# Two-layer transformer kernel: second-layer key chunks of 3, 4, 4, 3, 2 tiles, clock-keeping filler in dead score banks, and one key tile in sixteen exponentiated on VectorE

## The chip, the cores and the metric

The kernel runs on one core of a Trainium2 chip. Every time is device time in microseconds (us) of one execution; a kernel's time is the median of its runs. A profile is one further execution, so its span differs a little from the median.

Names: PE is TensorE's matrix multiplications, PEld its weight loads, DVE is VectorE, ACT is ScalarE, POOL is GpSimd. PSUM is the memory that TensorE writes (eight banks of 512 fp32 columns); SBUF is the memory beside all engines. PV stands for the product of the probabilities with the values.

## The reference, cut to what matters

```python
def _A_ref(x, wqkv, wo):                 # S = 2048 rows, D = 448, 16 heads of 28
    q, k, v = split_heads(x @ wqkv)
    scores = einsum("bhqd,bhkd->bhqk", q, k) * (28 ** -0.5)
    return merge_heads(einsum("bhqk,bhkd->bhqd", softmax(scores), v)) @ wo

def _B_ref(x, w1, w2, w3, w4):
    h = gelu(layernorm(x) @ w1)          # 448 wide, then shifted by rows -1, +1, -2, +2
    x1 = x + shifted(h) @ w2
    return x1 + gelu(layernorm(x1) @ w3) @ w4      # 1792 wide

x = A_x
x = x + _A_ref(layernorm(x), ...);  x = x + _B_ref(layernorm(x), ...)
x = x + _A_ref(layernorm(x), ...);  x = x + _B_ref(layernorm(x), ...)   # same weights again
```

Two layers with the same weights. The second layer's attention needs keys from every row of the first layer's output, so there is a **seam**: the second layer can only begin on the keys that the first layer's MLP has already finished.

## The kernel before: the parts that the change and the argument touch

The work is written as tasks (Python generators), one per stage. When the program is built, a small planner simulates them with estimated durations and priorities and so fixes one order of instructions for each engine. Each engine is given its list in that order, and the profiles show it: in those of the changed kernel and of runs 5 and 6, the 1230 instructions of VectorE, the 882 of ScalarE and the 394 of GpSimd come in one and the same order.

```python
def c_ps(n): return 0.07 + n * 0.00104        # planner's estimate: VectorE, n columns from PSUM;
                                              # used for four of the five operations of t_dexp too

# rows are cut in 16 tiles of 128. (first tile, tiles) of the query chunks, and per layer the
# order of the segments: (query chunk, from key tile, to key tile)
CHUNKS = {0: [(0,4),(4,4),(8,4),(12,4)], 1: [(0,4),(4,4),(8,4),(12,2),(14,2)]}
ORDER = {0: [(0,0,4),(0,4,8),(0,8,16),(1,0,16),(2,0,16),(3,0,16)],
         1: [(0,0,4),(0,4,8),(1,0,8),(0,8,12),(1,8,12),(0,12,16),(1,12,16),
             (2,0,16),(3,0,16),(4,0,16)]}     # each times 4 head groups of 4 heads

def DVE_TILES(L, ch, g, p): return 0          # key tiles of a segment exponentiated on VectorE
def MIXP(L, ch): ...                          # priority of a query chunk's out-projection and MLP
def KVP(L, c): ...                            # priority of a key chunk's projections; low = early
```

A **block** is one head, one tile of 128 keys and up to 512 queries: one PSUM bank. ScalarE takes two or three blocks in one exponential. `t_dexp` is the same thing on VectorE; it was in the kernel before, but its list was empty:

```python
def t_exp():                                                   # ScalarE
    for u, un in enumerate(units):
        yield ("wait", ("st", u))                              # scores are in PSUM
        if u >= 6:                                             # its PT slot is read by PV of unit u-6
            for (si, kb, j) in units[u - 6]: yield ("wait", ("pv", si, kb))
        yield op("act", 0.07 + n * 0.427, ... activation(out=PT[...], in_=ps[...], func=ACT.Exp, scale=SCALE))
        ...
def t_dexp(w):                                                 # VectorE: exp by exponent bits and a cubic
        ...
        b = yield ("acq", MISC, [("yd", w)])                   # one of the spare PSUM banks
        yield from score_ops([blk], [bi(b)])
        op("dve", ... tensor_scalar(out=y, in0=ps[:, bi(b), :], ..., op0=ALU.mult, op1=ALU.max))
        op("dve", ... scalar_tensor_tensor(out=q, in0=lo, ..., in1=lo, ...))    # lo, hi: halves of y
        op("dve", ... scalar_tensor_tensor(out=q, in0=q, ..., in1=lo, ...))
        op("dve", ... tensor_scalar(out=pd, in0=q, ..., op0=ALU.mult, op1=ALU.add))
        op("dve", ... scalar_tensor_tensor(out=pd, in0=hi, scalar=128.0, in1=pd, ...))
        ...
def t_pv():                                                    # one PSUM bank (5), one segment at a time
    for si in range(len(segs)):
        if si > 0: yield ("wait", ("ucopied", si - 1))         # bank 5 copied out
        while todo or dtodo:
            if dtodo and (not todo or <its VectorE blocks are done>):  ... read PD
            else:                                                      ... read PT
```

The keys of a chunk pass through projection, a square (ScalarE for the very first, GpSimd otherwise), a sum and a maximum; from the maximum comes the **bias** that keeps the exponentials in range. A segment with new keys waits for that bias.

```python
fast = L == 0 and c == 0 and g == 0                            # square on ScalarE
...
def keep_pe_busy(self, until):                                 # filler between two PE instructions
    dur, fn, banks, key, reads = self.fill                     # banks: ["b6", "b7"], the spare ones
    while self.cur["pe"] + dur + 0.12 < until:
        used = <planned TensorE work in the last WIN us>
        if used > self.TARGET * self.WIN: ...continue          # quota reached
        for b in banks:
            if self.busy.get(b, False): continue
            ...
        self.P.add("pe", <small matmul into bank b>)
```

## Time and profile before

The three runs took 1208.27 us (1207.6 to 1210.52).

| | span us | ScalarE busy | exponentials | VectorE busy | GpSimd busy | mean granted clock |
|---|---|---|---|---|---|---|
| before | 1202.5 | 1059.7 | 819, 939.3 us | 452.2 | 382.7 | 0.956 |

The prediction below shows the rows that name the bound. Three more lines of the page matter later: VectorE's row of the 40 slices, the score matmuls, and GpSimd's normalisation. A group's line ends in its busy time, the mean ns of one instruction, the idle time of its engine before it, and what ended most of it.

```profile
DVE  8464213331242235331643353423352433233243
...
L1138 PE MATMUL ps<-qT,kT 32*128 32x512 bf16 (+1 forms) x2304 | 326.5, 368 | 52.2 <-ACT PT L1213 43.6
...
L850 POOL TENSOR_SCALAR xn<-x_res,mv,mst 128x448 bf16<-128x448 f32 x30 | 55.6, 1865 | 1.9 <-DVE mst L1451 1.9
```

VectorE is far from full (most slices 1 to 5 tenths). The score matmuls wait mostly for an exponential to release their bank (43.6 of 52.2 us), which is what a ScalarE bound looks like from TensorE. The windows view of the stretch at the seam gives each engine's busy time in 45 us (columns: PE, PEld, DVE, ACT, POOL, granted clock, DMA share, GB/s); ScalarE works only 26.65 of them:

```profile
690.00:735.00 45.00, 39.88 (x462) 15.29 (x455) 23.36 (x58) 26.65 (x25) 12.19 (x13) 0.93 0.20 61
```

### The profile page before, as it was taken

How to read it: one execution, taken by the hardware profiler on the slowest of the kernel's cores; microseconds unless marked ns; L12 is line 12 of the kernel's file. 1: busy time of each engine (PE TensorE's matmuls, PEld its weight loads, DVE VectorE, ACT ScalarE, POOL GpSimd, SP SyncE). 2: the span in 40 equal slices, each digit the busy share in tenths (PEclk: the TensorE clock that was granted, in tenths of full speed). 3: DMA queues.
4: the chain of work that ended last, by engine and by line, in shares of the span. 5: the costliest groups of instructions: out<-in, count | busy, mean ns of one | idle time of the engine just before them, and what ended most of it. 6: DMA issues, size and time to landing. Idle time of an engine off the chain costs nothing.

```text
span 1202.5 us, 34008 instructions
## 1 busy us (share of the span) xinstructions
PE 1058.9 (88%) x15542; PEld 417.7 (35%) x15542; DVE 452.2 (38%) x921; ACT 1059.7 (88%) x906; POOL 382.7 (32%) x396
## 2 busy tenths in 40 slices
PE   5998888889888899898988998988889898889888
PEld 2333333343323332223332433332323433334355
DVE  8464213331242235331643353423352433233243
ACT  3768999999989999989999958998989999899932
POOL 4931114403325054412343240202427501252201
PEclk9899999899979999998998999998999998899899
DMA  3384112002111032011231021324321110220000
GB/s 102 83 242 103 38 51 46 15 17 71 27 30 29 11 107 46 11 19 48 75 94 35 20 90 44 106 89 112 60 38 35 26 45 22 45 47 11 10 17 22
DMA packets 95784, 64.28 MB, mean 53 GB/s; under 512 B 64664, under 2 KB 84440, under 8 KB 95640
## 3 DMA queue, kind: packets, MB, share of 16 engines
q1 hardware_dynamic: 92376, 57.63, 19.2%
q0 software_dynamic: 2304, 3.67, 1.2%
q8 instruction: 122, 2.00, 0.7%
q10 hardware_dynamic: 960, 0.80, 0.2%
q14 instruction: 22, 0.18, 0.1%
HBM read 28.16 MB, written 16.76 MB: 37 GB/s over the span
## 4 chain that ended last, share of the span: by engine, by line
ACT 40%; PE 37%; DMA 8%; DVE 7%; POOL 5%; issue 1%; SPq 0%; ACTq 0%; POOLq 0%; DVEq 0%
ACT PT L1213 34%; PE ps L706 21%; PE ps L1138 9%; PE ps L697 6%; DMA rb<-rscr 4%; ACT h2T L1604 3%; POOL xn L850 2%; DMA xT<-xnd 1%; POOL otn L1357 1%; ACT hT L1488 1%; DMA rscr<-rT 1%; PE ps L1643 1%; DVE kmaxc L981 1%; DMA rT<-ub 1%; ACT L1604 1%
## 5 line engine op out<-in xcount | busy, mean ns | idle before, releaser
L1213 ACT ACTIVATE PT<-ps 128x1536 bf16<-128x1536 f32 (+1 forms) x819 | 939.3, 1307 | 59.2 <-PE ps L1138 56.6
L1138 PE MATMUL ps<-qT,kT 32*128 32x512 bf16 (+1 forms) x2304 | 326.5, 368 | 52.2 <-ACT PT L1213 43.6
L697 PE MATMUL ps<-PT,vaug 128*32 128x512 bf16 (+1 forms) x2304 | 254.1, 367 | 2.0 <-DVE ub L1335 2.0
L1138 PEld LDWEIGHTS ps<-qT,kT 32*128 32x128 bf16 x2304 | 80.3, 91 | 342.6 <-ACT PT L1213 271.7
L1643 PE MATMUL ps<-wq_pad,ident 128*32 128x256 bf16 x3836 | 182.4, 282 | 2.1 <-DVE x1b L1547 1.0
L706 PE MATMUL ps<-xT,w 128*32 128x512 bf16 (+1 forms) x2240 | 173.2, 367 | 6.9 <-issue 4.7
L706 PE MATMUL ps<-w,h2T 128*32 128x448 bf16 x1792 | 123.5, 382 | 20.8 <-ACT h2T L1604 20.8
L1357 POOL TENSOR_TENSOR otn<-ub,rb 128x512 bf16<-128x512 f32 (+1 forms) x32 | 38.6, 1205 | 320.6 <-DMA rb<-rscr 314.1
L1643 PEld LDWEIGHTS ps<-wq_pad,ident 128*32 128x32 bf16 x3836 | 108.9, 98 | 43.3 <-issue 23.8
L1594 DVE CAST h2T<-ps 128x512 bf16<-128x512 f32 (+2 forms) x126 | 73.9, 586 | 121.0 <-PE ps L706 112.6
L697 PEld LDWEIGHTS ps<-PT,vaug 128*32 128x32 bf16 x2304 | 69.8, 95 | 102.1 <-issue 85.4
L706 PEld LDWEIGHTS ps<-xT,w 128*32 128x32 bf16 x2240 | 59.0, 96 | 63.8 <-issue 38.1
L706 PEld LDWEIGHTS ps<-w,h2T 128*32 128x32 bf16 x1792 | 49.7, 102 | 68.6 <-issue 27.3
L850 POOL TENSOR_SCALAR xn<-x_res,mv,mst 128x448 bf16<-128x448 f32 x30 | 55.6, 1865 | 1.9 <-DVE mst L1451 1.9
L958 POOL TENSOR_TENSOR sq<-qT 128x512 bf16<-128x512 bf16 x31 | 32.1, 1040 | 73.0 <-DVE qT L1001 68.8
L850 POOL TENSOR_SCALAR xn<-x1b,mv,mst 128x448 bf16<-128x448 f32 x29 | 54.5, 1879 | 1.7 <-POOL mst L1553 0.2
L1333 DVE COPY ub<-ps 128x512 f32<-128x512 f32 (+1 forms) x36 | 22.7, 630 | 85.4 <-PE ps L697 85.2
L958 POOL TENSOR_TENSOR sq<-kT 128x512 bf16<-128x512 bf16 x31 | 32.2, 1041 | 66.6 <-DVE kT L970 63.5
L706 PE MATMUL ps<-w,hT 112*32 112x448 bf16 x512 | 40.9, 414 | 13.8 <-ACT hT L1488 13.5
L706 PE MATMUL ps<-xT,wq_pad 128*32 128x512 bf16 x512 | 44.8, 420 | 6.2 <-DMA xT<-xnd 5.5
L706 PE MATMUL ps<-wo_pad,otn 128*32 128x448 bf16 x512 | 42.0, 378 | 9.1 <-POOL otn L1357 6.1
L1604 ACT ACTIVATE h2T<-h2T 128x7168 bf16<-128x7168 bf16 (+2 forms) x9 | 45.1, 5015 | 3.9 <-DVE h2T L1594 3.8
(134 smaller groups left out, 869.4 us busy)
## 6 DMA issues: line engine op xcount, KB each, us to landing
uscr<-ub SPq DMA_DIRECT2D x28, 256.0 KB
ub<-uscr SPq DMA_DIRECT2D x28, 256.0 KB
rb<-rscr SPq DMA_DIRECT2D x28, 256.0 KB
xnd<-xn SPq DMA_DIRECT2D x28, 128.0 KB, 2.0
x_res<-in_A_x_dram POOLq DMA_DIRECT2D x16, 224.0 KB, 3.5
xd<-x_res SPq DMA_DIRECT2D x16, 224.0 KB, 2.1
x_res<-xd SPq DMA_DIRECT2D x16, 224.0 KB
out_dram<-obf SPq DMA_DIRECT2D x16, 112.0 KB
```

Source lines behind the costliest of these rows:

```text
L697: return lambda e: e.matmul(out=out, lhsT=lhsT, rhs=rhs, start=start, stop=stop, **kw)
L706: r.append(e.matmul(out=out[c:c + w, :], lhsT=lhsT[:, c:c + w], rhs=rhs, start=start, stop=stop, tile_position=(0, c)))
L850: yield op(eng, dur, lambda e: e.tensor_scalar(out=xn[:, k, 0:D], in0=src, scalar1=scalar1, scalar2=scalar2, op0=ALU.subtract, op1=ALU.mul ...
L958: return op("pool", 1.2, lambda e: e.tensor_tensor(out=sq[:, si, :], in0=src, in1=src, op=ALU.mult), reads=rk, writes=[("sq", si)])
L981: yield op("dve", c_ps(512), lambda e: e.reduce_max(out=kmaxc[:, L, g, c:c + 1], in_=ps[:, bi(b2), :], axis=AX.X), reads=[("ps", bi(b2))], ...
L1138: yield op("pe", max(0.055, 0.22 / nc_ * NW / 512.0), lambda e, i=i, kc=kc, j=j, g=g, a=a, NW=NW, bank=bank: e.matmul(out=ps[:, bank, i * ...
L1213: yield op("act", 0.07 + n * 0.427, lambda e, bk=bk, s0=s0, n=n: e.activation(out=PT[:, s0:s0 + n, :], in_=ps[:, bk[0]:bk[0] + n, :], func ...
L1333: yield op("dve", c_ps(NW), lambda e: e.tensor_copy(out=u, in_=ps[:, 5, 0:NW]), reads=[("ps", 5)], writes=[uk])
L1357: yield op("pool", 0.2 + NW * 0.0021, lambda e: e.tensor_tensor(out=otn[:, g, 0:NW], in0=u, in1=rb[:, 0:NW], op=ALU.mult), reads=[uk, ("rb ...
L1594: ev = op("dve", c_ps(NW), lambda e, fch=fch, b=b: e.tensor_copy(out=h2T[:, fch, 0:NW], in_=ps[:, bi(b), 0:NW]), reads=[("ps", bi(b))], wr ...
L1604: yield op("act", c_act(14 * NW), lambda e: e.activation(out=h2T[:, :, 0:NW], in_=h2T[:, :, 0:NW], func=ACT.Gelu_apprx_tanh), reads=allk, ...
L1643: return [e.matmul(out=ps[32 * c:32 * c + 32, bi(b), 0:256], lhsT=ident[:, 32 * c:32 * c + 32], rhs=wq_pad[:, 0, 0:256], start=True, stop= ...
```

## The change

It aims at ScalarE from several sides: fewer exponentials for it (VectorE takes one key tile in sixteen of each full segment), earlier keys at the seam (chunks that end where the MLP's groups of tiles end, and new priorities), a better clock (filler in more banks), a shorter start (first squares on ScalarE), and planner estimates nearer to the trace. The core of the diff:

```diff
-    WIN = 3.42                          # filler window and quota
-    TARGET = 0.5
+    WIN = 2.3
+    TARGET = 0.52
-                if self.busy.get(b, False):
+                if b not in self.dead:
-        SC.fill = (0.12, filler, ["b6", "b7"], ...)
+        SC.fill = (0.12, filler, ["b6", "b7", "b0", "b1", "b2", "b3", "b4"], ...)

 def DVE_TILES(L, ch, g, p):
-    return 0
+    return {16: 1}.get(p, 0)

 MIXP: -(0, 3): 1.6                      +(0, 3): 1.4
 KVP:  -(1, 1): 1.5, (1, 2): 1.5         +(1, 1): 2.5, (1, 2): 2.5, (1, 4): 1.5

-        return 0.07 + n * 0.00104       # c_ps
+        return 0.13 + n * 0.00108
 # ... and small VectorE operations estimated at 0.2 instead of 0.1 or 0.12

-  1: [(0,0,4),(0,4,8),(1,0,8),(0,8,12),(1,8,12),(0,12,16),(1,12,16),(2,0,16),...]
+  1: [(0,0,7),(1,0,7),(0,7,11),(1,7,11),(0,11,16),(1,11,16),(2,0,16),...]
+    KC = {0: [(0,4),(4,4),(8,4),(12,4)], 1: [(0,3),(3,4),(7,4),(11,3),(14,2)]}
 # ... projections, squares and maxima take 128 * n columns instead of 512

-            fast = L == 0 and c == 0 and g == 0
+            fast = L == 0 and c == 0
-            if idx == 0 and g == 0:     # the same for the first queries' squares
+            if idx == 0:
 # ... banks b4 and b3 are left out of the general list until the tail (MISC[0:3]); a query projection
 #     waits for its bias before it takes a bank; bookkeeping of dead banks cut
```

## The prediction

> **What bounds the kernel now.** The median is 1208.27 us; the profiled execution spans 1202.5 us. I read the page first, then the groups of instructions, then ScalarE's timeline, then the waits and the PE timeline around ScalarE's gaps.
>
> ```profile
> span 1202.5 us, 34008 instructions
> PE 1058.9 (88%) x15542; PEld 417.7 (35%) x15542; DVE 452.2 (38%) x921; ACT 1059.7 (88%) x906; POOL 382.7 (32%) x396
> ACT  3768999999989999989999958998989999899932
> PEclk9899999899979999998998999998999998899899
> L1213 ACT ACTIVATE PT<-ps 128x1536 bf16<-128x1536 f32 (+1 forms) x819 | 939.3, 1307 | 59.2 <-PE ps L1138 56.6
> L1643 PE MATMUL ps<-wq_pad,ident 128*32 128x256 bf16 x3836 | 182.4, 282 | 2.1 <-DVE x1b L1547 1.0
> ```
>
> TensorE and ScalarE look equally full at 88%, but 182.4 us of TensorE is filler (line 1643) that only keeps its clock up. ScalarE does no filler: 939.3 of its 1059.7 us are the softmax exponentials of line 1213. In the ACT row most slices are 9s; the holes are the start (3, 7, 6), the 5 in slice 24 (690 to 720 us) and the last two slices. So ScalarE is the bound, with 1202.5 - 1059.7 = 142.8 us idle.
>
> The price of an exponential comes from a long undisturbed stretch, and the largest hole from the same view, ScalarE's timeline (start, duration, line, shapes, count, idle before and its releaser):
>
> ```profile
> 683.35 1.28 ACT L1604 ACT_TABLE_LOAD   x1
> 684.64 4.68 ACT L1604 ACTIVATE h2T<-h2T 128x5376 bf16<-128x5376 bf16 x1
> ...
> 694.26 13.94 ACT L1213 ACTIVATE PT<-ps 128x1536 bf16<-128x1536 f32 x12 [1.26 <-PE ps L1138]
> 722.52 0.20 ACT L1113 ACTIVATE fct<-dbc 128x4 f32<-128x4 f32 x1 [14.32 <-DVE dbc L1108]
> 723.63 4.86 ACT L1213 ACTIVATE PT<-ps 128x1536 bf16<-128x1536 f32 x4 [0.91 <-PE ps L1138]
> ...
> 783.88 0.27 ACT L1113 ACTIVATE fct<-dbc 128x4 f32<-128x4 f32 x1
> ...
> 1055.32 63.50 ACT L1213 ACTIVATE PT<-ps 128x1536 bf16<-128x1536 f32 x56
> ```
>
> The last line: 63.50 us for 56 exponentials, 1.134 us each. They alternate between 3 and 2 blocks (a block is one head, one tile of 128 keys, 512 queries), so 2.5 on average: **0.4536 us a block**. The 14.32 us line is the seam between the layers: ScalarE has run out of second-layer keys and waits for the bias step of a new key chunk.
>
> **What the skill says.** (1) "ScalarE: Activation LUTs", section What ACT_TABLE_LOAD costs, gives 0.833 ns per element; a block of 512 would then be 0.427 us plus its part of a fixed cost. The 0.4536 us agrees, and its table load of about 1283 ns is the 1.28 us line. (2) "VectorE: DVE Perf Modes", section Why PSUM operands drop a tier: fp32 read from PSUM runs at one element a cycle. The trace agrees: 512 columns from PSUM take 691 ns (the h2T cast of line 1594), where a bf16 scalar op inside SBUF takes 347 ns (line 1160). (3) "TensorE: Matmul & The Clock Gate", section Part 1: idleness of about 3.4 us drops the clock to half. The trace shows that after a gelu:
>
> ```profile
> 547.08 3.77 PE L1643 MATMUL ps<-wq_pad,ident 128*32 128x256 bf16 x124
> 554.24 5.42 PE L706 MATMUL ps<-w,h2T 128*32 128x448 bf16 x56 [3.39 <-ACT h2T L1604]
> 559.59 0.45 PE L1138 MATMUL ps<-qT,kT 32*128 32x512 bf16 x3
> ```
>
> The filler planned over the 7.5 us of table load and gelu runs off in 3.77 us, TensorE idles 3.39 us, and the granted clock in 556 to 560 us is 0.53.
>
> **The change part by part.**
>
> *One key tile in sixteen on VectorE.* It holds for segments of 16 key tiles whose query chunk is 4 tiles wide: chunks 1, 2, 3 of layer one and chunk 2 of layer two (chunks 3 and 4 there are 2 wide and excluded). That is 4 chunks x 4 head groups = 16 segments, each with 1 key tile x 4 heads: 64 of the 2048 blocks (2 x 16 heads x 16 key tiles x 4). ScalarE loses 64 x 0.4536 = **29.0 us**, and its 819 exponentials become about 794 (1984 / 2.5). This lies on the bound nearly everywhere: from 165 to 290 us ScalarE is busy 122 of 125. VectorE pays five operations a block: one from PSUM (0.69), three two-tensor ones inside SBUF (0.70 to 0.74, as the neighbours on lines 1027 and 1335), one fp32 to bf16 scalar op (about 0.42, between 347 ns and the PSUM price), together about 3.25 us. 64 x 3.25 = 208 us, so VectorE goes from 452 to about 660 us. In 290 to 430 us it is busy 39 of 140; 16 blocks add 52, giving 65%. It stays beside ScalarE. The score matmul uses the row group that a 3-block unit leaves free. The price is coupling: a block holds one of the two spare PSUM banks, projections wait for VectorE behind 0.7 us operations, and the last PV of a segment waits for the chain. I put that at one VectorE operation, about 0.6 us, per segment: 16 x 0.6 = **+10 us**.
>
> *Key chunks of 3, 4, 4, 3, 2 tiles.* The first layer's MLP finishes tiles in groups 0-2, 3-6, 7-10, 11-13, 14-15. Now chunk 2 is tiles 8 to 11, so it waits for the group of 11-13, whose gelu ends at 689 us. ScalarE has only 256 blocks (64 + 64 + 128) to do before that. The new chunks end where the groups end: 2 x 7 x 16 + 2 x 4 x 16 = 352 blocks need nothing from the last query chunk. Between 690 and 735 us ScalarE is busy 26.65 of 45: 18.35 us idle, which this part attacks. But the new order needs keys 11 to 15 together, all five chunks, and earlier in the work. First-layer exponentials end at about 575 us (the 410th). 352 x 0.4536 = 159.7 us, plus three gelu interruptions in that stretch (4.5, 7.3, 5.8), bring ScalarE to 752 us; the bias of the last keys came at 784 us. The chain must become 32 us shorter. The priorities help: the last chunk's MLP goes from 1.6 to 1.4 while second-layer key projections go from 1.5 to 2.5, so the out-projection (598 to 612 us, amid key and query work) and the last MLP groups no longer stand behind them, and the last key step is 2 tiles instead of 4 (765 to 784 us). I estimate 25 of the 32 us, so a new stall of about 7: net **-11 us**. Segments of layer two go from 40 to 36; those in the short round have 20 blocks instead of 16, so the normalisation chain behind it (rb from DRAM, 824 to 880 us, 11 us of ScalarE idle) gets more room: **-3 us**.
>
> *Filler in dead score banks, window 2.3 us.* Filler may use any bank whose contents are dead, instead of only the two spare ones. The gaps after gelu stay: the filler there has reached its quota already, and its quota rises only from 50 to 52%. Gaps from a late transpose DMA (TensorE waits 2.8 us for xT at 827 us, then runs at half clock) are not filler's to mend, as the planned DMA times are unchanged. I give it **-4 us**. It is also needed because the VectorE blocks occupy the two banks filler used.
>
> *Start.* All four head groups of the first chunk square on ScalarE instead of three of them on GpSimd (1.04 us each, six in all). ScalarE is idle 26 us between 23.6 and 109 us, so the six squares (6 x 0.6 = 3.6 us busy) fit, and they shorten the wait of 10.92 us at 25 us by about 3: **-3 us** of span.
>
> *VectorE cost estimates* are nearer to the trace (0.69 for 512 columns from PSUM instead of 0.60); they cost nothing and make the order fit better. I give them no number.
>
> Sum: -29 + 10 - 11 - 3 - 4 - 3 = **-40 us: 1168 us**.
>
> **Rivals.** (a) *VectorE becomes a second bound.* For it: second-layer chunk 2 has its blocks where VectorE is already busy 30.6 of 65 us (880 to 945); with 52 us over some 120, it reaches about 85%, and every PSUM evacuation queues. Against it: only one stage is so full. If it held, half of the 29 us would come back: about 1185 us. (b) *The seam moves instead of closing.* If the chain to keys 11-15 does not get shorter, ScalarE stalls 32 us at one point instead of 18 spread out: 14 us worse than before, so 1193 us. For it: much of that chain is latency (GpSimd normalising four tiles, 7.4 us; transpose DMAs). Against it: the priorities were retuned for it. (c) *Everything falls in place*: seam fully hidden, coupling near zero, filler removes half of the 39 us of small waits for scores: -29 - 18 - 3 - 15 - 3 = -68, 1140 us.
>
> **Range and chances.** (a) and (c) stand about as far off on either side; (b) is the worst single one. I take 1143 to 1193. Faster by over 2% means under 1184.1 us: the 29 us saved on ScalarE alone reach 1179, so only a new wait prevents it: 0.79. Within 2%: 0.18; slower: 0.03.
>
> **What would show it.** ScalarE: about 794 exponentials, total busy about 1034 us. VectorE about 660 us, still with idle time in each stage. The seam: no wait of 14 us on the bias near 700 us, and at most a short one before the (11-16) segments. Granted clock dips still after gelus. The prediction is wrong if ScalarE's idle time grows above 143 us: then look for waits of score matmuls on VectorE, or PV matmuls on the VectorE blocks, in chunks 1 to 3 of layer one.

## The result, and the profile after

The changed kernel took **1162.23 us** (1159.99 to 1165.16), with a ratio of **0.9629** to the kernel before (95% interval 0.9586 to 0.9672): faster. Ratios here are the mean time of one kernel's fast runs over that of the other's of the same rounds, so they are not quite the ratio of the medians quoted. In another session, on a kernel before of 1206.37 us, the same kernel took 1162.77 us at 0.965.

The page of the changed kernel, first the span, then the engines' busy times, three rows of the 40 slices, the exponentials and the filler:

```profile
span 1158.2 us, 33576 instructions
PE 1028.3 (89%) x15190; PEld 404.7 (35%) x15193; DVE 642.4 (55%) x1230; ACT 1026.0 (89%) x882; POOL 400.6 (35%) x394
...
DVE  7754237775677786756663424513658764333352
ACT  4958999999899999797799999899989999999922
PEclk9989999999899999999999999999989999999999
...
L1233 ACT ACTIVATE PT<-ps 128x1536 bf16<-128x1536 f32 (+2 forms) x794 | 906.1, 1322 | 53.4 <-PE ps L1158 37.7
...
L1665 PE MATMUL ps<-wq_pad,ident 128*32 128x256 bf16 x3416 | 155.6, 277 | 7.0 <-DVE yd L1269 3.2
```

ScalarE is still the fullest engine that does no filler. It has 33.7 us less work (1059.7 to 1026.0), but only 10.6 us less idle time (142.8 to 132.2). The ACT row has new holes in slices 17, 19 and 20 (7 where 9 stood, between 463 and 579 us); they are the subject of most of what follows. VectorE's row more than doubled between slices 7 and 20 (the digits add up to 91 instead of 41).

The seam, from ScalarE's timeline (start, duration, line, count, in brackets the idle time before and its releaser). The small exponential `fct` is the step behind the bias of the last keys:

```profile
748.43 0.20 ACT L1133 ACTIVATE fct<-dbc 128x4 f32<-128x4 f32 x1 [4.02 <-DVE dbc L1128]
749.54 48.48 ACT L1233 ACTIVATE PT<-ps 128x1024 bf16<-128x1024 f32 x43 [0.90 <-PE ps L1158]
```

The 14.32 us wait of before is gone; one of 4.02 + 0.90 us remains.

To see where the time went I count exponentials in each trace and so cut it into phases: the first 128 blocks; the rest of the first layer; the split segments of the second layer (query chunks 0 and 1); its full segments; and the tail after the last exponential. In us, each row from the one profiled execution of its kernel:

| kernel | first 128 blocks | rest of layer 1 | split segments | full segments | tail | span |
|---|---|---|---|---|---|---|
| before | 104.3 | 472.0 | 279.0 | 290.7 | 56.5 | 1202.5 |
| after | 100.7 | 457.9 | 264.8 | 272.1 | 62.7 | 1158.2 |
| after without VectorE tiles | 102.6 | 468.9 | 255.8 | 286.9 | 53.7 | 1167.9 |
| after with old key chunks | 101.8 | 463.5 | 276.5 | 269.3 | 62.3 | 1173.4 |
| after with old estimate | 98.6 | 466.6 | 260.5 | 283.3 | 63.7 | 1172.7 |
| after, no VectorE tiles in layer 1's last query chunk | 100.9 | 450.6 | 257.8 | 275.1 | 63.1 | 1147.5 |

In the rest of layer 1, VectorE took 48 blocks, which at the 0.4536 us of the prediction are 21.8 us of ScalarE; the phase shrank by 14.1. So a part of the gift was lost just there. How far one row may be trusted: a second profile of the changed kernel gave 100.3, 462.1, 264.7, 273.2 and 62.7, and the profiled execution of the kernel without VectorE tiles was the slowest of its four (1170.92 us; the others 1154.77 to 1165.07).

### The profile page after: what moved, and what is told of

It is laid out like the page before. It is cut to its first block, busy times and chain, and to the rows that moved or that the text cites. A ratio compares the mean times of both kernels' runs of the same rounds, so it can differ in the third digit from the quotient of the medians.

```text
span 1158.2 us, 33576 instructions
## 1 busy us (share of the span) xinstructions
PE 1028.3 (89%) x15190; PEld 404.7 (35%) x15193; DVE 642.4 (55%) x1230; ACT 1026.0 (89%) x882; POOL 400.6 (35%) x394
## 4 chain that ended last, share of the span: by engine, by line
ACT 54%; PE 26%; DVE 7%; DMA 6%; POOL 4%; SPq 1%; issue 1%; ACTq 0%; DVEq 0%
ACT PT L1233 47%; PE ps L720 14%; PE ps L1158 6%; PE ps L711 5%; ACT h2T L1626 3%; DMA rb<-rscr 2%; POOL xn L864 2%; ACT L1233 1%; ACT hT L1510 1%; DMA xT<-xnd 1%; DVE h2T L1616 1%; DMA rT<-ub 1%; POOL otn L1379 1%; DVE qd L1272 1%; ACT L1626 1%
## 5 line engine op out<-in xcount | busy, mean ns | idle before, releaser
L1233 ACT ACTIVATE PT<-ps 128x1536 bf16<-128x1536 f32 (+2 forms) x794 | 906.1, 1322 | 53.4 <-PE ps L1158 37.7
L720 PE MATMUL ps<-xT,w 128*32 128x512 bf16 (+2 forms) x2240 | 173.8, 365 | 8.2 <-DVE h2T L1616 2.3
L1665 PE MATMUL ps<-wq_pad,ident 128*32 128x256 bf16 x3416 | 155.6, 277 | 7.0 <-DVE yd L1269 3.2
L1379 POOL TENSOR_TENSOR otn<-ub,rb 128x512 bf16<-128x512 f32 (+1 forms) x32 | 40.4, 1262 | 267.5 <-DMA rb<-rscr 255.8
L1665 PEld LDWEIGHTS ps<-wq_pad,ident 128*32 128x32 bf16 x3416 | 93.3, 97 | 42.6 <-issue 18.6
L720 PEld LDWEIGHTS ps<-xT,w 128*32 128x32 bf16 (+1 forms) x2240 | 60.9, 96 | 64.6 <-issue 30.8
L864 POOL TENSOR_SCALAR xn<-x_res,mv,mst 128x448 bf16<-128x448 f32 x30 | 62.1, 2076 | 1.9 <-DVE mst L1473 1.5
L972 POOL TENSOR_TENSOR sq<-kT 128x512 bf16<-128x512 bf16 (+2 forms) x32 | 30.6, 957 | 89.9 <-DVE kT L986 76.7
L864 POOL TENSOR_SCALAR xn<-x1b,mv,mst 128x448 bf16<-128x448 f32 x29 | 57.2, 1973 | 1.7 <-POOL mst L1575 0.2
L1357 DVE SCALAR_TENSOR_TENSOR ub<-ub,fct,ps 128x512 f32<-128x512 f32 x24 | 17.9, 747 | 71.9 <-PE ps L711 69.9
L720 PE MATMUL ps<-xT,wk_pad 128*32 128x512 bf16 (+2 forms) x576 | 47.2, 375 | 6.8 <-DMA xT<-xnd 5.8
L1573 POOL TENSOR_SCALAR mst<-mv 128x1 f32<-128x1 f32 x32 | 8.0, 259 | 120.3 <-DVE mv L850 120.2
```

Source lines behind the costliest of these rows:

```text
L720: r.append(e.matmul(out=out[c:c + w, :], lhsT=lhsT[:, c:c + w], rhs=rhs, start=start, stop=stop, tile_position=(0, c)))
L864: yield op(eng, dur, lambda e: e.tensor_scalar(out=xn[:, k, 0:D], in0=src, scalar1=scalar1, scalar2=scalar2, op0=ALU.subtract, op1=ALU.mul ...
L972: return op("pool", 0.15 + NW * 0.0018, lambda e: e.tensor_tensor(out=sq[:, si, 0:NW], in0=src, in1=src, op=ALU.mult), reads=rk, writes=[( ...
L1233: yield op("act", 0.07 + n * 0.427, lambda e, bk=bk, s0=s0, n=n: e.activation(out=PT[:, s0:s0 + n, :], in_=ps[:, bk[0]:bk[0] + n, :], func ...
L1357: yield op("dve", c_ps(NW), lambda e: e.scalar_tensor_tensor(out=u, in0=u, scalar=fct[:, L, p[1], g:g + 1], in1=ps[:, 5, 0:NW], op0=ALU.mu ...
L1379: yield op("pool", 0.2 + NW * 0.0021, lambda e: e.tensor_tensor(out=otn[:, g, 0:NW], in0=u, in1=rb[:, 0:NW], op=ALU.mult), reads=[uk, ("rb ...
```

## The experiments

Each edit has the planner fix a new order of instructions, so a run changes the part named and small things elsewhere. Differences of some 3 us are therefore not put down to a part. No run re-planned the kernel after an edit without meaning, so how much a new order alone can do was not measured.

**First question: which part carries the gain?** My theory was the prediction's sum, with the VectorE tiles as its largest term; the rival was that the seam and the order of work carry it.

**1. The VectorE tiles taken away** (three rounds).

```diff
-    return {16: 1}.get(p, 0)
+    return 0
```

> The changed kernel with no key tile on VectorE (819 exponentials on ScalarE again). Theory A (the 29 us that ScalarE was spared were half given back by the two waits of 7.5 and 7.0 us at ends of first-layer chunk-3 segments): 1172 to 1184 us, no wait of ScalarE on a PV matmul over 2 us. Rival B (the part is worth its full 29 us, the waits would be there anyway): 1188 to 1194 us. Rival C (coupling eats all of it): 1160 to 1166 us.

Measured: 1164.2 us, ratio 0.967 (0.9608 to 0.9731). The changed kernel has 0.9629 and 0.965. Of 1205 us that is 2 to 5 us, with overlapping intervals, where the prediction had -19; rival C's range has it. Its ScalarE is busy 1058.8 us, 33 more than with the tiles, so the tiles do take the work off ScalarE; the time is lost again elsewhere. By phase, the tiles gain 11.0 us in the rest of layer 1 and 14.8 in the full segments, and lose 9.0 in the split segments and 9.0 in the tail. (In the tail a gelu of 8.7 us with its two table loads moved behind the last exponential, so that loss is the other side of part of the 14.8.) These differences are not the tiles' alone: another order without VectorE tiles (run 11) has 458.1 in the rest of layer 1 and 264.3 in the split segments, the same as the changed kernel with them.

**2. The VectorE tiles alone, on the kernel before** (three rounds).

```diff
-    return 0
+    return {16: 1}.get(p, 0)
```

> The kernel before with only the VectorE key tile turned on (794 exponentials). Theory A: gains 10 to 20 us on 1208, so 1188 to 1198 us, with new waits at ends of first-layer chunk-3 segments and the 14 us seam wait still there. Rival B (full 29 us): about 1179 us. Rival C (nothing without the rest of the change, because filler and VectorE blocks compete for the two spare banks): 1203 to 1213 us.

Measured: 1220.79 us, ratio **1.0109** (1.0036 to 1.0182). Alone, the largest term of the prediction makes the kernel slower by 13 us, which is under 2% and outside all three ranges. ScalarE's busy time fell to 1028.0 us; its idle time rose to 192.8. The waits view has 78.5 us of waits for score matmuls (56.6 in the kernel before), 33.1 on the bias (26.3) and 18.0 for PV (none), the last at 483 and 522 us, in layer 1's last query chunk.

**3. The old key chunks, order and priorities in the changed kernel** (three rounds).

```diff
-    KC: 1: [(0,3),(3,4),(7,4),(11,3),(14,2)]
+    KC: 1: [(0,4),(4,4),(8,4),(12,4)]
 # ORDER of layer 2 and the slots of its keys as before
 # KVP (1,1), (1,2): 2.5 -> 1.5;  MIXP (0,3): 1.4 -> 1.6
```

> The changed kernel with the second layer's key chunks, segment order and priorities of before. Theory A (the seam part is worth about 12 us): 1171 to 1179 us, with a wait of 14 us or more on the bias near the seam. Rival (the change's gain comes from VectorE, filler and better estimates; chunks only move the wait): 1160 to 1166 us.

Measured: 1175.75 us, ratio 0.9779 (0.9739 to 0.982): 16 to 18 us slower than the changed kernel, most of it (11.7 us by the phases) in the split segments. The wait on the bias is back, from ScalarE's timeline:

```profile
708.73 0.20 ACT L1133 ACTIVATE fct<-dbc 128x4 f32<-128x4 f32 x1 [16.46 <-DVE dbc L1128]
```

**Where do the VectorE tiles lose it?** The waits view names what ScalarE waited for (total us, times, longest). An exponential waited for a PV matmul twice in the changed kernel, and never in the one without VectorE tiles:

```profile
ACT PT L1233 <- PE ps L711: 14.5, 2, 7.5
```

Both stand behind the end of a segment of layer 1's last query chunk (number 3): the first in the chunk, the second just after its last segment, where ScalarE is already 14 blocks into the second layer and so, in the table above, in the split segments. A gelu waits between them. From ScalarE's timeline:

```profile
491.59 27.52 ACT L1233 ACTIVATE PT<-ps 128x1536 bf16<-128x1536 f32 x24 [7.52 <-PE ps L711]
...
526.84 6.18 ACT L1626 ACTIVATE h2T<-h2T 128x7168 bf16<-128x7168 bf16 x1 [6.43 <-DVE h2T L1616]
...
571.13 36.43 ACT L1233 ACTIVATE PT<-ps 128x1536 bf16<-128x1536 f32 x32 [6.96 <-PE ps L711]
```

What TensorE did in the first of these gaps (its timeline, 484 to 492 us):

```profile
484.12 0.60 PE L1158 MATMUL ps<-qT,kT 32*128 32x512 bf16 x3
...
488.13 0.40 PE L720 MATMUL ps<-sq,astat 128*32 128x512 bf16 x4 [1.45 <-POOL sq L972]
488.36 0.38 PE L711 MATMUL ps<-PD,vaug 128*32 128x512 bf16 x2
...
489.95 0.39 PE L711 MATMUL ps<-PD,vaug 128*32 128x512 bf16 x2 [1.10 <-DVE PD L1278]
490.27 0.66 PE L1158 MATMUL ps<-qT,kT 32*128 32x512 bf16 x2
491.16 1.04 PE L711 MATMUL ps<-PT,vaug 128*32 128x512 bf16 x14 [0.22 <-DVE k L1113]
```

Between 484.7 and 490.3 us no score matmul is issued. The list holds, in this order, a step of the second layer's keys that waits for GpSimd's square, then the last PV matmuls of a segment on a VectorE block (`PD`), the last of them waiting for VectorE's fifth operation. Only behind them come scores, VectorE's copy of the PV bank, then the PV matmuls on `PT` (491.16) whose end gives ScalarE its next slot. In the 7.52 us, TensorE waits 1.45 for the square and 1.10 for `PD`, after 1.49 us of filler (from 485.18 us). And why VectorE was late, from its timeline and GpSimd's beside it:

```profile
484.39 0.74 DVE L986 TENSOR_SCALAR kT<-ps,cols 128x512 bf16<-128x512 f32 x1
485.05 0.68 DVE L1269 TENSOR_SCALAR yd<-ps 128x512 int32<-128x512 f32 x1
...
487.21 1.15 DVE L1276 TENSOR_SCALAR PD<-qd 128x512 bf16<-128x512 f32 x1
488.39 1.50 DVE L1278 SCALAR_TENSOR_TENSOR PD<-yd,PD 128x512 int16<-128x512 int16 x1
...
490.42 0.68 DVE L1355 COPY ub<-ps 128x512 f32<-128x512 f32 x1
```
```profile
486.64 1.43 POOL L972 TENSOR_TENSOR sq<-kT 128x512 bf16<-128x512 bf16 x1
488.04 1.31 POOL L1584 TENSOR_TENSOR x_res<-x_res,x1b 128x448 f32<-128x448 f32 x1
```

VectorE ran the chain without a gap, behind a second-layer key (485.05 follows 484.39), so it had no slack; and its last two operations, beside GpSimd's, took 1.15 and 1.50 us where their means are 0.487 and 0.742. While ScalarE works on this query chunk (410.6 to 558.6 us) VectorE is busy 105.21 of 148.0 us with exponentials, the second layer's keys and queries, and the MLP; before (437.9 to 576.3 us), 52.40 of 138.4. In run 3, with VectorE as busy (107.48 of 144.1), ScalarE loses the time in another place: one gelu waits 15.47 us for VectorE, and PV only 2.1.

**4. VectorE tiles everywhere but in layer 1's last query chunk** (three rounds). If the theory holds, giving those 16 blocks back to ScalarE costs it 16 x 0.4536 = 7.3 us and removes about 21 us of waits.

```diff
 def DVE_TILES(L, ch, g, p):
+    if L == 0 and ch == 3: return 0
     return {16: 1}.get(p, 0)
```

> The changed kernel without VectorE key tiles in the first layer's chunk 3 only (12 segments instead of 16, 800 exponentials). Theory A (in chunk 3 VectorE is busy with the second layer's keys, so the VectorE blocks finish late and PV waits for them: 7.5 + 7.0 + a gelu wait of 6.4 us): 16 blocks return to ScalarE (+7.3 us), the waits go (about -20 us): 1147 to 1154 us, faster than the changed kernel. Rival (the waits come from elsewhere): 1167 to 1171 us.

Measured: **1149.81 us, ratio 0.9567** (0.9516 to 0.9618). ScalarE has more work than in the changed kernel (1034.6 us busy against 1026.0) and the kernel is faster. The waits are gone from its timeline, and VectorE is busy 56.45 of 140.0 us in the chunk. Of the same session's run 1, without any VectorE tile, it is 12 us ahead by the ratios: 12 VectorE segments do gain. No run took four segments from another query chunk instead.

```profile
466.16 65.07 ACT L1235 ACTIVATE PT<-ps 128x1536 bf16<-128x1536 f32 x57
531.25 1.28 ACT L1628 ACT_TABLE_LOAD   x1
532.54 6.18 ACT L1628 ACTIVATE h2T<-h2T 128x7168 bf16<-128x7168 bf16 x1
538.74 1.28 ACT L1235 ACT_TABLE_LOAD   x1
540.03 61.67 ACT L1235 ACTIVATE PT<-ps 128x1024 bf16<-128x1024 f32 x54
```

**Second question: what are the other parts worth?** The next runs shared the kernel before at 1206.37 us, with five rounds each.

**5. The changed kernel again**, for the same session.

> The changed kernel again, unaltered, as the yardstick of this job: 1158 to 1167 us by every theory.

Measured: 1162.77 us, ratio 0.965 (0.962 to 0.968).

**6. The old filler** (the order of all other instructions stays).

```diff
-    WIN = 2.3;  TARGET = 0.52;  banks b6, b7, b0 to b4
+    WIN = 3.42; TARGET = 0.5;   banks b6, b7
```

> The changed kernel with the filler of before: banks b6 and b7 alone, window 3.42 us, target 0.50. All other instructions keep their order on every engine. Theory A (filler is worth about 4 us, as predicted): 1163 to 1170 us, a slightly lower granted clock. Rival (filler is what explains the 15 to 20 us that VectorE, seam and start leave unexplained, because the VectorE blocks take the two spare banks away from it): 1175 to 1185 us with a granted clock near 0.95.

Measured: 1163.03 us, ratio 0.9662 (0.963 to 0.9694): 1.4 us by the ratios, with overlapping intervals, so no effect that I can measure. The mean granted clock was 0.972 with the old filler and 0.976 with the new one, with 308 matmuls fewer.

**7. The old estimate of a VectorE operation on PSUM.** No instruction is changed by this, only the order.

```diff
-        return 0.13 + n * 0.00108
+        return 0.07 + n * 0.00104
```

> The changed kernel ordered with the old estimate of a VectorE operation on PSUM (0.60 us for 512 columns in place of 0.68). Theory A (no number, as predicted): 1158 to 1168 us. Rival (the nearer estimates are what makes the static order fit the chip and explain the unexplained 15 to 20 us): 1172 to 1185 us, with more waits of ScalarE for score matmuls of under 3 us.

Measured: 1178.45 us, ratio **0.9789** (0.9755 to 0.9824): 17 us slower than the changed kernel of the same session, from a part to which the prediction gave no number. In the profiles ScalarE's waits for PV grow from 14.8 us (changed kernel, same session) to 24.5, and those for score matmuls from 42.4 (38 times) to 48.4 (43 times). The mean granted clock of its six runs is 0.962, against 0.979; whether that is a cause of the loss or a trace of TensorE's idle time, no run separates. This is the first of the two waits for PV (13.50 and 11.0 us) in its timeline, now in query chunk 2:

```profile
334.58 11.41 ACT L1233 ACTIVATE PT<-ps 128x1536 bf16<-128x1536 f32 x10 [13.50 <-PE ps L711]
```

**8. The old squares at the start.**

```diff
-            fast = L == 0 and c == 0            /  if idx == 0:
+            fast = L == 0 and c == 0 and g == 0 /  if idx == 0 and g == 0:
```

> The changed kernel with only the first head group squaring on ScalarE, the other three on GpSimd as before. Theory A: the first 51 exponentials end 3 to 4 us later and the time rises by as much: 1165 to 1168 us. Rival (the start is hidden later, or the six squares on ScalarE cost what they save): 1159 to 1164 us.

Measured: 1168.11 us, ratio 0.9702 (0.9667 to 0.9737): about 6 us slower. The first 128 blocks end at 103.6 us instead of 100.3 in the same session, so 3.3 us are at the start itself, where the prediction had 3; the rest comes later, and I did not find out where.

**Third question: do the estimates matter because of the VectorE tiles, and do the priorities carry the seam?** The last runs shared the kernel before at 1202.14 us.

**9. The best version again** (five rounds).

> The version without VectorE key tiles in the first layer's chunk 3, again, as the best so far and as the yardstick of this job: 1146 to 1155 us, and below the changed kernel's ratio of 0.963 to 0.965.

Measured: 1150.86 us, ratio 0.956 (0.9524 to 0.9595). It beats both kernels in two sessions: by the ratios 8 to 11 us faster than the changed one.

**10. The best version with the old priorities** (three rounds): the new key chunks stay.

```diff
-    KVP (1,1), (1,2): 2.5;  MIXP (0,3): 1.4
+    KVP (1,1), (1,2): 1.5;  MIXP (0,3): 1.6
```

> That version with the priorities of before (last first-layer MLP 1.6, second-layer keys 1.5) and the new key chunks. Theory A (the chunk bounds alone do not close the seam: the priorities shorten the chain to keys 11 to 15): a wait of 18 to 25 us on the bias before the (11-16) segments in place of 3.8 us, and 1163 to 1173 us. Rival (the bounds do it alone): 1147 to 1155 us with a wait under 8 us.

Measured: 1169.08 us, ratio 0.9725 (0.9689 to 0.976), 20 us slower than run 9. The wait on the bias is larger than the kernel before ever had:

```profile
754.55 0.20 ACT L1135 ACTIVATE fct<-dbc 128x4 f32<-128x4 f32 x1 [18.29 <-DVE dbc L1130]
```

In run 9 that wait is 3.75 us. From the end of the first layer's exponentials to this point 199.6 us pass here, and 183.4 us with the new priorities. So new chunks without new priorities are rival (b): the seam moves and does not close. In run 3, with old chunks and old priorities, the same stretch takes 202.4 us, so what shortened it was mostly the priorities. Old chunks with the new priorities were not run; whether the new chunks are needed at all is open.

**11. The old estimate without VectorE tiles** (five rounds).

```diff
-    return {16: 1}.get(p, 0)   ->  return 0
-    c_ps: 0.13 + n * 0.00108   ->  0.07 + n * 0.00104
```

> The changed kernel without VectorE key tiles and with the old estimate of a VectorE operation on PSUM. Theory A (the nearer estimate matters because VectorE is loaded with exponentials): 1161 to 1170 us, near the 1164 us of the run without VectorE tiles. Rival (the estimate makes any order fit the chip better, worth its 16 us regardless): 1175 to 1185 us.

Measured: 1166.98 us, ratio 0.971 (0.9678 to 0.9741). Run 1, the same with the new estimate, has 0.967: some 5 us, with overlapping intervals, so not distinguishable from 0. With the tiles the estimate was worth 17.

**12. The VectorE tiles on the kernel before, with the new estimate** (three rounds).

```diff
-    DVE_TILES: return 0        ->  return {16: 1}.get(p, 0)
-    c_ps: 0.07 + n * 0.00104   ->  0.13 + n * 0.00108
```

> The kernel before with the VectorE key tile and the new estimate of a VectorE operation on PSUM. Theory A (the VectorE tile lost time on the kernel before because its order was made with the old estimate): 1190 to 1203 us instead of the 1221 us without the new estimate. Rival (it lost because of the old seam and the old filler): 1213 to 1226 us.

Measured: 1203.03 us, ratio 1.0007 (0.997 to 1.0044). Against run 2 the estimate gains 12 us; against the kernel before, tiles and estimate together gain nothing. ScalarE's waits for PV stay, at 15.0 us after 18.0; its waits for score matmuls fall from 78.5 to 68.6.

## Why the prediction was right or wrong

**The time was right.** 1168 us were predicted, 1162 measured; -40 us predicted, and by the medians -44 (1206.37 to 1162.77) to -46 (1208.27 to 1162.23) measured. But part of this is luck: the tile term was 14 to 17 us too large and the term without a number was about as much too small. The terms must be read one by one.

| term of the sum | predicted us | measured us, by taking it back |
|---|---|---|
| VectorE tiles, with coupling | -29 + 10 = -19 | -2 to -5 |
| seam: chunks, order, priorities | -11 - 3 = -14 | -16 to -18 |
| filler | -4 | -1.4, not distinguishable from 0 |
| start | -3 | -6 |
| estimates | no number | -17 (`c_ps` alone) |

The measured column adds up to about 45, but that is not a proof that the parts are independent. Runs 1, 7 and 11 speak against it: the estimate is worth 17 us with VectorE tiles and some 5 without. The estimates of the small operations, the two banks left out and the wait before query projections were not taken back.

**The bound: right.** ScalarE does no filler and stayed the fullest engine. The 794 exponentials came out exactly. Their line fell by 33.2 us (939.3 to 906.1) where 64 x 0.4536 = 29.0 was predicted.

**VectorE's cost: right.** The five operations of a block, from the groups by shape:

```profile
L1272 DVE SCALAR_TENSOR_TENSOR qd<-yd 128x512 f32<-128x512 uint16 x64 | 49.0, 776 | 0.4
L1278 DVE SCALAR_TENSOR_TENSOR PD<-yd,PD 128x512 int16<-128x512 int16 x64 | 46.9, 742 | 0.5
L1274 DVE SCALAR_TENSOR_TENSOR qd<-qd,yd 128x512 f32<-128x512 f32 x64 | 45.9, 725 | 0.3
L1269 DVE TENSOR_SCALAR yd<-ps 128x512 int32<-128x512 f32 x64 | 42.8, 678 | 2.1 <-PE ps L1158 2.0
L1276 DVE TENSOR_SCALAR PD<-qd 128x512 bf16<-128x512 f32 x64 | 30.5, 487 | 0.4
```

They add up to 3.41 us where 3.25 was predicted, and VectorE ended at 642.4 us busy where 660 was. (The prediction called its neighbours on lines 1027 and 1335 operations inside SBUF; both read PSUM.)

**The coupling: right mechanism, wrong size and shape.** The step was "I put that at one VectorE operation, about 0.6 us, per segment: 16 x 0.6 = +10 us". "The last PV of a segment waits for the chain" is what the trace shows, but not as 0.6 us everywhere. In the segments of the other query chunks no exponential waits for PV at all; behind segments of layer 1's last chunk two waits of about 7 us stand, with a gelu wait of 6.43 us between. Rival (a) looked for the crowded stage in the second layer's chunk 2 (its 85% is nearer 90: 30.6 of 65 and 52 of 120 are 47% and 43%), though the prediction's last sentence names PV on VectorE blocks in layer one as a place to look. It was layer 1's last query chunk, where VectorE also takes the second layer's keys and queries from PSUM. Run 4 shows this: without those 16 blocks the waits are gone and the kernel gains 8 to 11 us although ScalarE does more. The tiles that stay are then worth about 12 us (runs 1 and 4).

**The failed step: "they cost nothing and make the order fit better. I give them no number".** The estimates were the part with no term, and taking one of them back costs 17 us. The planner prices four of a block's five VectorE operations with this estimate and the fifth at 0.34 us: 2.75 us a block with the old estimate, 3.07 with the new, 3.41 on the chip. That a wrong order is the way from there to the loss is argued, not shown: TensorE's list says where a PV matmul on a VectorE block stands, the planner puts it where it thinks that VectorE is done, and an estimate that is too short puts it too early. The longer PV waits of run 7 and the small effect in run 11, where there are no such blocks, agree with this. But in the gap before run 7's first wait (321.1 to 334.6 us) TensorE waits for VectorE eight times, 4.6 us in all, and only 0.59 us of it is at the `PD` matmul; and in run 12 the gain lies more in the waits for scores than in those for PV. What the runs show is that the estimate's worth depends on the tiles (17 and 12 us with them, some 5 without); in the prediction the tiles carry 19 us and the estimate none.

**The seam: right, a little too small.** The chain had to become 32 us shorter and I gave it 25. From the end of the first layer's exponentials to the bias of the last keys it took 207.6 us before (576.3 to 783.9) and 189.8 after (558.6 to 748.4): 17.8 shorter. The new stall was put at 7 and was 4.92 us (4.02 + 0.90). The misses cancel: I had put ScalarE's own stretch at 177 us (752 - 575), and it took 185.8 (558.6 to the start of the wait at 744.4). The argument for the priorities held: run 10 shows that without them the new chunks lose 20 us. What the chunk bounds add to the priorities was not separated.

**The filler: too large.** "I give it -4 us": between runs 6 and 5 the clock rose by 0.004 and the time did not change measurably. Most of the rise from the 0.956 of the kernel before is there with the old filler too (0.972). I had no basis for a number.

**The start: right in place, too small in all**, 3.3 us at the start and 6 in the whole.

**Still open.** The tail after the last exponential grew from 56.5 to 62.7 us; one gelu that the planner moved behind the last exponential accounts for it in the timeline, but no run moved only that gelu. Of the 9.0 us by which the split segments are longer than in run 1, although they hold no VectorE tile, 6.96 are the second wait for PV, which layer 1's last VectorE block causes there; it goes away in run 4, where the phase is 7.0 us shorter. In run 9 the chain to the last keys' bias is 6.4 us shorter too (189.8 to 183.4). By what way the estimate costs time is open, as said above.

## What to carry to other kernels

Work moved from a full engine to a half-empty one is not free in a stage where that engine is busy with something that others wait for; look at its load stage by stage, and leave those stages out: here 48 blocks on VectorE beat 64 by 8 to 11 us. In a statically ordered program, the estimates behind the order are part of the kernel: when an engine becomes loaded, correct its estimates from the trace first, and give that correction a term of its own when you predict. A new cut of the work along a chain of latencies needs the priorities of that chain with it, or the wait only moves (run 10); whether the priorities alone would have done it here, no run shows.

## What the Trainium skill lacked or had wrong

- "SBUF — State Buffer", section Who interferes with whom, says that VectorE instructions with two SBUF inputs, or in the two-port modes, contend with GpSimd (with two inputs, where the GpSimd instruction reads SBUF), and that the one that comes second blocks. The trace agrees in part: the fp32 to bf16 scalar operation took 1.15 us and the int16 two-tensor one 1.50 us beside GpSimd operations of 1.43 and 1.31 us. Counted over the changed kernel's profile by starts and durations, the three two-tensor operations of a chain (L1272, L1274, L1278) took 0.682, 0.675 and 0.683 us with no GpSimd instruction beside them (at most 0.694) and 0.849, 0.778 and 0.813 with one (up to 1.76), but 73 of these 96 took no longer than 0.694, so most overlaps cost VectorE nothing; the scalar one (L1276) 0.417 and 0.575; the one that reads PSUM (L1269) 0.678 both ways. The page lacks what this comes to in a mixed stream: GpSimd's normalisation (the L850 line, L864 after) went from 1.865 to 2.076 us a tile. That it is the tiles, runs show: 1.864 and 1.860 without them (runs 1 and 11), 2.042 with them alone on the kernel before (run 2).
- "VectorE: DVE Perf Modes", section The perf-mode tier table, has no row for an operation of two tensors and a scalar, and no page gives a time for it. For 512 columns inside SBUF, with no GpSimd instruction beside it, the changed kernel's profile shows means of 0.675 us (fp32), 0.683 us (int16, one input with stride two) and 0.682 us (16-bit input with stride two, fp32 out): 16-bit data brought nothing in these forms.
- "TensorE: Matmul & The Clock Gate", section Part 1: The HAM clock gate, explains why filler is wanted, but not what more of it is worth once the clock is mostly up: here 308 more filler matmuls raised the mean clock from 0.972 to 0.976 and gave 1.4 us of 1163, within the scatter.
- No page has the cost of one late instruction in a fixed order across engines: behind a segment whose last PV matmuls read a VectorE block, ScalarE was idle for 7.52 us, though TensorE's own waits for GpSimd and VectorE in that gap were 1.45 and 1.10; with the old estimate the longest such gap was 13.50.
